# A fused Fourier mixing and SoLU block in fp32: a transform moved one step, the last units' sums and products moved to other engines

## The chip, the cores and the metric

The kernel runs on one core of one Trainium2 chip. The metric is device time in microseconds of one execution, the median over several runs. The five engines that appear are TensorE (PE, with its weight loads as PEld), VectorE (DVE), ScalarE (ACT), GpSimd (POOL) and SyncE (SP); SP only issues DMAs here.

## The reference

The reference mixes eight sequences of 3136 rows and 256 features with a two-dimensional Fourier transform, of which the real part is kept, and then applies an MLP with a SoLU activation and a layer norm. All is fp32.

```python
X = np.fft.fft(x, axis=1)             # x: (8, 3136, 256)
X = np.fft.fft(X, axis=2).real
h = X.reshape(25088, 256) @ w_in      # (256, 1024)
sm = softmax(h)                       # exp(h - max) / sum
solu = h * sm
ln = (solu - mean) / sqrt(var + 1e-6) * g_ln
out = ln @ w_out                      # (1024, 256)
```

## The kernel before

**Pairs and units.** Two sequences form a pair; there are four pairs. The row index of a sequence is split as 49 x 64. A first transform (`transform1`, L176) works over the 49, one piece of it for two of the 64 columns; its result z is written to a DRAM tile `zd` (`keep`, L215) and read back with other axes in the partitions as `g` (`turn`, L218: four DMAs for each group of five k1). A second transform (`transform2`, L226) makes for each of 25 values of k1 one unit; the k1 and 49 - k1 rows of the output come from the sum and the difference of two halves, called signs 1 and 0. A unit of k1 = 0 has one sign alone. So there are 100 units, numbered through: 25 to each pair.

**One unit.** `up` (L259) multiplies q (the second transform's result, copied by ACT at L242) with `Wi` on PE, in four matmuls of 512 columns, which are two records each in the profile (L264). DVE makes ev (`even`, L267) and then both signs' h with their maxima (`join`, L273); ACT takes the exponential (`expo`, L281), DVE the product h times exp (`product`, L289), ACT the squares for the variance (`square`, L296). DVE transposes in blocks of 32 (`turn_both`, L334, L336), and sixteen DMAs on SP carry the blocks to their places in `uT` (`move_blocks`, L358, L365), for two units at a time. The unit's small statistics follow on ACT (`stats`, L303) and as a power on POOL (`power`, L313, L316).

**Down projection.** The output of a unit with two signs is a product of a 2 x 2 block matrix with a 2 x 2 block matrix. Class `Down` (L403) computes it with seven block products of four 128-column matmuls each (`product7`, L398, L401) instead of eight. For this, four sums S of blocks of uT are formed on POOL (`sums`, L388, L394), about 1.3 us each, into one of two S tiles. The products lie in shared PSUM banks: C11 in bank 2, X in bank 3, the pair P4 and P5 in bank 1. `seed` (L426) copies C11 into X on ACT before p6 accumulates there; `keep_p`, `keep_x` and `keep_c` scale results out of the banks on ACT, and `finish` (L455) adds the rest on DVE. Units with one sign, the first units and the last unit use plain products with `Wo` instead (`down`, L462, L468) and a scale on ACT (L473). Results leave by one plain DMA on SP and, for sign 1, by one indirect DMA on POOL (`store`, L475).

**Order.** The program's order is written out by hand under a manual schedule; each engine runs its own instructions in that order. Units 0 to 4 (`whole = 4`) run in a first loop: the units before unit 4 are transposed by PE (`turn_whole`, L341), whose second half of PSUM copies is on DVE (L790). From unit 5 on, step i of the second loop holds `up` of unit i, the down projection of unit i - 5 (`lag = 5`), the sums of unit i - 4, and the elementwise work of unit i. After unit 99, steps 100 to 105 drain the pipeline. Bank 0 (L199, L233) serves the second transform and the first transform's pieces in turn, so a piece of `transform1` waits until ACT has copied q out.

**The next pair's work.** While pair p runs, `ahead` (L641) prepares pair p + 1. For each of eight chunks c it adds the mirrored rows on POOL in two halves (`add_mirror`, L128, L134), folds the features on DVE in two halves (`fold_part`, L156, L141, L142, L166) with a small copy on ACT (L167), and loads chunk c + 2 (`load`, L109: one DMA on SP at L117 and an indirect one on POOL at L119). `ahead_pe` puts two pieces of `transform1` per chunk on PE (L208). Chunk c's first mirrored half stands in step `SUMS[p][c]`, that is base + 2c with a base for each pair; the folds stand in that step + 1 and + 2, the load in + 2, and the pieces of the transform in + 3 and + 4. `turn_parts` (L664) reads the five groups of g at steps -4, -3, 2, 6 and 11 of the pair, on POOL's queue, into three buffers. The block moves of two units are issued in even steps, before that step's loads.

A mirrored sum and the first sum of S wait for the product of an earlier unit; `behind` adds that wait:

```python
def behind(i, t):
    tc.add_manual_dep(i.ins, t.last.ins.name, ...,
[...]
```

Of the kernel before, what the change touches and what calls it, by code (L numbers as in the profile page):

```python
# [26 lines left out]
NC = NH // CH  # L27
# [8 lines left out]
def kernel(  # L36
# [19 lines left out]
    nc = tc.nc  # L56
    B, S, D = x.shape
# [70 lines left out]
    def add_mirror(pr, c, engine, part=None):  # L128

        xa, xb, _ = pr.raw[c]  # L130
        rows = (0, CH) if part is None else (part * CH // 2, (part + 1) * CH // 2)
        r = slice(rows[0], min(rows[1], CH - 1 if c == NC - 1 else CH))
        a, rb = xa[:, r, :], xb[:, ::-1, :][:, r, :]
        i = engine.tensor_tensor(out=a[:, :, 1:D], in0=a[:, :, 1:D], in1=rb[:, :, D - 1 : 0 : -1], op=ALU.add)  # L134
        if part is None:
            engine.tensor_tensor(out=a[:, :, 0:1], in0=a[:, :, 0:1], in1=rb[:, :, 0:1], op=ALU.add)
        return i
# [143 lines left out]
    def expo(t, s):  # L281
        if s == 0:
            t.esum = small.tile([P, 2], FP32, tag="esum", name="esum")
            t.both = fpool.tile([P, 2, FF], FP32, tag="u", name="u", bufs=1)
        t.u[s] = t.both[:, s]
        nc.scalar.activation(out=t.u[s], in_=t.h[s], func=ACT.Exp, bias=t.nmax[:, s : s + 1], scale=-1.0,  # L286
                             accum_out=t.esum[:, s : s + 1])
# [8 lines left out]
    def square(t, s):  # L296

        if s == 0:
            t.ssq = small.tile([P, 2], FP32, tag="ssq", name="ssq")
        nc.scalar.activation(out=t.h[s], in_=t.u[s], func=ACT.Square, bias=t.usum[:, s : s + 1], scale=-float(FF),  # L300
                             accum_out=t.ssq[:, s : s + 1])
# [32 lines left out]
    def turn_both(t):  # L334
        if len(t.signs) == 2:
            nc.vector.transpose(out=t.batch.v[:, t.w].rearrange("p f o -> p o f"), in_=t.both)  # L336
        else:
            for s in range(2):
                turn_blocks(t, s)
# [45 lines left out]
    def blocks_of(t):  # L385
        return [S_tiles[t.w][:, j] for j in range(4)]

    def sums(t, prv):  # L388

        A11, A12, A21, A22 = blocks(t)  # L390
        S = blocks_of(t)
        for j, a, b, op in ((0, A21, A22, ALU.add), (1, S[0], A11, ALU.subtract), (3, A12, S[1], ALU.subtract),
                            (2, A11, A21, ALU.subtract)):
            i = nc.gpsimd.tensor_tensor(out=S[j], in0=a, in1=b, op=op)  # L394
            if j == 0 and prv:
                behind(i, prv)

# [238 lines left out]

    SUMS = [None] + [[f + 2 * c for c in range(NC)] for f in (3, 28, 53)]

    def ahead(pr, i, work):  # L641

        for c in range(NC):
            a = i - SUMS[pr.p][c]
            if work == "load" and (i == (pr.p - 1) * NK and c < 2 or a == 2 and c + 2 < NC):
                load(pr, c if a != 2 else c + 2)
            if work == "mirror" and a in (0, 1):
                behind(add_mirror(pr, c, nc.gpsimd, a), units[i - 1])
            if work == "fold" and a in (1, 2):
                fold_part(pr, c, a - 1)  # L650

    def behind(i, t):

        tc.add_manual_dep(i.ins, t.last.ins.name,
                          mybir.DependencyInfo(mybir.DependencyClass.Sync, mybir.DependencyReason.DATA),
                          reason="two operands at a time from SBUF")
# [7 lines left out]

    def turn_parts(pr, step):

        at = (-4, -3, 2, 6, 11)
        if step in at:
            turn(pr, at.index(step))

    with tc.manual_schedule():
# [71 lines left out]
        units = [Unit(p, k1) for p in range(NP) for k1 in range(NK)]  # L743
# [7 lines left out]
        lag = 5  # L751
        whole = 4
# [21 lines left out]
        def other_pairs(i, do, *a):  # L774
            cur = units[i]
            if cur.p + 1 < NP:
                do(pairs[cur.p + 1], i, *a)
# [3 lines left out]
        for i in range(whole + 1):  # L781
            cur = units[i]
            prv = units[i - 1] if i else None
            if prv:
                turn_whole(prv)
            for s in cur.signs:
                join(cur, s)
            if prv:
                for o, ps in prv.wait:
                    nc.vector.tensor_copy(out=o, in_=ps)  # L790
            for s in cur.signs:
                expo(cur, s)
            if i == 0:

                weights.narrow_out(3)
            for s in cur.signs:
                product(cur, s)
                if i < whole and s == 0:
                    square(cur, s)
            if i == 1:  # L800
                weights.centre()
                weight_sums()
            if i < whole:

                begin(i + 1)
                if 1 in cur.signs:
                    square(cur, 1)
                stats(cur)
                power(cur)
            else:  # L810
                for s in cur.signs:
                    square(cur, s)
                turn_both(cur)
                stats(cur)
                power(cur)
            if i == 0:
                turn(first, 1, nc.sync)
            for work in ("mirror", "fold", "load"):
                other_pairs(i, ahead, work)

        def by_seven(i):

            return 0 <= i < len(units) - 1 and len(units[i].signs) == 2

# [1 line left out]
        for i in range(whole + 1, len(units) + lag + 1):  # L828
            cur = units[i] if i < len(units) else None
            prv = units[i - 1] if whole < i - 1 < len(units) else None  # L830
            old = units[i - lag] if i < len(units) + lag else None
            seven = by_seven(i - lag)
            kept = units[i - lag - 1] if i >= lag + 1 else None

            if kept:
                store(kept, 0)
            if cur:
                enter(i)
                even(cur, up(cur, 0))
                cur.odd = up(cur, 1)  # L840
                second_transform(i + 2)
            if seven:
                new = Down(old, fresh)
                fresh = False
                new.p1()
                new.seed()
            if prv:
                stats(prv)
            if seven:
                new.p4()  # L850
                new.p5()
                new.keep_p()
            elif old:
                plain = [(s, down(old, s, result(s + 1)[:, 0:D])) for s in old.signs]
            if cur:
                other_pairs(i, ahead_pe)
            if seven:
                new.p6()
                new.keep_x()
                new.p2()  # L860
                new.keep_c()
            elif old:
                for s, ps in plain:
                    scale(old, s, ps)
            if cur:
                for s in cur.signs:
                    join(cur, s)
            if seven:
                new.p3()
                new.p7()  # L870
                new.finish()
            if cur:
                other_pairs(i, ahead, "mirror")
            if by_seven(i + 1 - lag):
                sums(units[i + 1 - lag], prv)
            if i % 2 == 0 and whole < i - 1 < len(units) - 2:
                batches[i // 2 - 1].place()
                move_blocks(batches[i // 2 - 1], slice(0, 2))
            if prv:
                power(prv)  # L880
            if kept and 1 in kept.signs:
                store(kept, 1)
            if cur:
                other_pairs(i, ahead, "fold")
                for s in cur.signs:
                    expo(cur, s)
                for s in cur.signs:
                    product(cur, s)
                for s in cur.signs:
                    square(cur, s)  # L890
                turn_both(cur)
                if cur.p == 0 and i in (5, 8, 11):
                    turn(first, (i + 1) // 3)
                for pr in pairs[1:]:
                    turn_parts(pr, i - pr.p * NK)
                other_pairs(i, ahead, "load")
            if i in (len(units), len(units) + 1):
                w = i - len(units)
                if w == 0:
                    batches[-1].place()  # L900
                move_blocks(batches[-1], slice(w, w + 1), (nc.sync, nc.gpsimd) if w else (nc.sync,))
# [76 lines left out]
```

## Time and profile before

| | us |
|---|---|
| median of 3 runs | 1172.91 |
| runs | 1169.1 to 1174.48 |
| the profiled execution | 1172.88 |
| its span | 1171.0 |
| PE busy | 1115.0 (95%) |
| DVE busy | 1022.6 (87%) |
| POOL busy | 868.2 (74%) |
| ACT busy | 757.5 (65%) |

The span begins with the first and ends with the last instruction of the profiled execution. Busy time counts an engine's instructions; in a line of the timeline stand the start, the duration, the engine, the line of the kernel, the operation, its tiles as out<-in, shapes and count, and in brackets the engine's idle time before it with what ended it. That last name is inferred, and of several causes the last one is named. In a line of windows stand the bounds, the length, each engine's busy time and count, the clock granted to TensorE as a share of full speed, the busy share of the DMA engines, and GB/s.

### The profile page before, as it was taken

Reading aid. Unit: us, or ns where it says so; the run is one execution under the profiler, and the core shown is the slowest. Engines: PE = TensorE matmul, PEld = TensorE weight load, DVE = VectorE, ACT = ScalarE, POOL = GpSimd, SP = SyncE. Lnnn points to the kernel's source line nnn. Section 1 sums busy time; section 2 is a strip of 40 time slices with the busy share of each in tenths; the row PEclk is TensorE's granted clock in tenths of the full one; section 3 lists DMA queues with packets and bytes.
Section 4 is the critical chain, followed back from the end, with each engine's and each line's share of the span. In section 5 each row is a group of like instructions: output and inputs, shape, how many; then the busy total and the mean of one; then the engine's idle time right before and its main releaser. Section 6 shows DMA issues by size and latency. Waiting matters only on the chain. (4 is left out here: it accounts for less than half of the span.)

```text
span 1171.0 us, 21594 instructions
## 1 busy us (share of the span) xinstructions
PE 1115.0 (95%) x7002; PEld 891.1 (76%) x7002; DVE 1022.6 (87%) x1428; ACT 757.5 (65%) x1721; POOL 868.2 (74%) x750
## 2 busy tenths in 40 slices
PE   2987999999999999999999999999999999999996
PEld 1555787787787777778878777878878788888886
DVE  7889989888999989999899999888898998998860
ACT  4566666667666666667666766676666666666651
POOL 3035888874998797887688889876598687777675
PEclk9999999999999989999999999999999999999998
DMA  9672798866897969886869797976596675956653
GB/s 240 197 190 45 168 186 186 196 144 145 157 182 155 186 149 174 170 174 143 161 133 202 156 190 164 205 174 144 134 168 154 130 161 113 165 120 134 137 120 93
DMA packets 458479, 185.75 MB, mean 159 GB/s; under 512 B 425750, under 2 KB 440350, under 8 KB 458368
## 3 DMA queue, kind: packets, MB, share of 16 engines
q1 hardware_dynamic: 444608, 146.22, 60.9%
q0 software_dynamic: 13760, 38.16, 12.5%
q8 instruction: 57, 0.93, 0.3%
q14 instruction: 54, 0.44, 0.1%
HBM read 44.78 MB, written 38.80 MB: 71 GB/s over the span
## 5 line engine op out<-in xcount | busy, mean ns | idle before, releaser
L264 PE MATMUL ps_h<-Wi,q 128*128 128x512 f32 x800 | 363.6, 596 | 11.4 <-DVE ev L270 5.9
L394 POOL TENSOR_TENSOR S<-uT 128x512 f32<-128x512 f32 x190 | 258.4, 1360 | 102.1 <-DMA r<-q 39.2
L300 ACT ACTIVATE h<-u,usum 128x1024 f32<-128x1024 f32 x196 | 225.2, 1149 | 155.8 <-DVE u L293 155.8
L401 PE MATMUL ps_m<-Ws,S 128*128 128x128 f32 x2280 | 297.3, 277 | 5.7 <-POOL S L394 3.3
L401 PEld LDWEIGHTS ps_m<-Ws,S 128*128 128x128 f32 x2280 | 280.0, 193 | 10.1 <-POOL S L394 3.7
L264 PEld LDWEIGHTS ps_h<-Wi,q 128*128 128x128 f32 x800 | 144.3, 191 | 160.0 <-issue 141.7
L293 DVE SCALAR_TENSOR_TENSOR u<-h,u 128x1024 f32<-128x1024 f32 x196 | 261.0, 1367 | 0.4 <-ACT u L286 0.3
L286 ACT ACTIVATE u<-h,nmax 128x1024 f32<-128x1024 f32 x196 | 223.7, 1143 | 19.3 <-DVE nmax L278 14.6
L336 DVE STREAM_TRANSPOSE v<-u 128x2048 f32<-128x2048 f32 x93 | 215.4, 2316 | 3.2
L401 PE MATMUL ps_m<-Wo,uT 128*128 128x128 f32 x1520 | 210.9, 282 | 0.0
L401 PEld LDWEIGHTS ps_m<-Wo,uT 128*128 128x128 f32 x1520 | 195.2, 197 | 0.9 <-issue 0.9
L394 POOL TENSOR_TENSOR S<-uT,S 128x512 f32<-128x512 f32 x95 | 134.9, 1420 | 7.4
L278 DVE CUSTOM_DVE_ANT_0 h<-ev,ps_h 128x1024 f32<-128x1024 f32 x100 | 122.1, 1221 | 18.1 <-DVE ev L270 7.4
L479 POOL DMA_INDIRECT out_dram<-ot,idx x96 | 115.6, 1204 | 29.4 <-issue 19.1
L394 POOL TENSOR_TENSOR S<-S,uT 128x512 f32<-128x512 f32 x95 | 129.1, 1359 | 7.5
L278 DVE CUSTOM_DVE_ANT_0 h<-h,ps_h 128x1024 f32<-128x1024 f32 x96 | 117.2, 1221 | 14.2 <-DVE nmax L278 0.5
L270 DVE SCALAR_TENSOR_TENSOR ev<-w_mid,r,ps_h 128x1024 f32<-128x1024 f32 x100 | 124.0, 1240 | 4.1 <-ACT S L530 2.6
L316 POOL TENSOR_TENSOR rs<-v,neg_half 128x2 f32<-128x2 f32 (+1 forms) x100 | 85.8, 858 | 32.3 <-ACT v L309 27.0
L401 PE MATMUL ps_m<-Ws,uT 128*128 128x128 f32 x760 | 105.0, 281 | 0.0
L208 PE MATMUL ps_m<-y,F 98*100 98x258 f32 (+3 forms) x288 | 73.8, 392 | 30.4 <-DVE y L154 23.1
L401 PE MATMUL ps_m<-Wo,S 128*128 128x128 f32 x760 | 100.9, 276 | 0.0
L236 PEld LDWEIGHTS ps_m<-T,g 128*128 128x128 f32 x400 | 60.2, 191 | 48.8 <-issue 46.0
(92 smaller groups left out, 1175.8 us busy)
## 6 DMA issues: line engine op xcount, KB each, us to landing
uT<-v SPq DMA_DIRECT2D x752, 128.0 KB
out_dram<-ot SPq DMA_DIRECT2D x100, 128.0 KB
g<-zd POOLq DMA_DIRECT2D x72, 160.0 KB, 5.2
xa<-in_x_dram SPq DMA_DIRECT2D x28, 392.0 KB
zd<-z SPq DMA_DIRECT2D x24, 400.0 KB
raw_in<-in_moe_w_in_dram SPq DMA_DIRECT2D x4, 512.0 KB
raw_out<-in_moe_w_out_dram SPq DMA_DIRECT2D x2, 1024.0 KB
r<-q SPq DMA_DIRECT2D x100, 0.5 KB
```

The costliest lines, as they stand in the source:

```text
L208: nc.tensor.matmul(o[..., cs], F[:, 2 * t + h, :], i[..., cs], start=first, stop=True, skip_group_check=True)
L264: nc.tensor.matmul(ps[:, fs], t.q[:, c * P : (c + 1) * P], Wi[:, c, fs], start=True, stop=True)
L270: nc.vector.scalar_tensor_tensor(out=t.ev, in0=w_mid, scalar=t.r, in1=ps, op0=ALU.mult, op1=ALU.add)
L278: nc.vector.tensor_tensor_reduce(out=t.h[s], in0=t.h[0] if s else t.ev, in1=t.odd, scale=1.0 if s else -0.5, scalar=3.0e38, op0=ALU.add, o ...
L286: nc.scalar.activation(out=t.u[s], in_=t.h[s], func=ACT.Exp, bias=t.nmax[:, s : s + 1], scale=-1.0, accum_out=t.esum[:, s : s + 1])
L293: t.last = nc.vector.scalar_tensor_tensor(out=t.u[s], in0=t.h[s], scalar=-1.0, in1=t.u[s], op0=ALU.mult, op1=ALU.mult, accum_out=t.usum[:, ...
L300: nc.scalar.activation(out=t.h[s], in_=t.u[s], func=ACT.Square, bias=t.usum[:, s : s + 1], scale=-float(FF), accum_out=t.ssq[:, s : s + 1])
L316: nc.gpsimd.tensor_tensor(out=t.rs[:, n], in0=t.v[:, n], in1=neg_half[:, n], op=ALU.pow)
L336: nc.vector.transpose(out=t.batch.v[:, t.w].rearrange("p f o -> p o f"), in_=t.both)
L394: i = nc.gpsimd.tensor_tensor(out=S[j], in0=a, in1=b, op=op)
L401: nc.tensor.matmul(o, a[:, c], b[:, c], start=start and c == 0, stop=c == n - 1, skip_group_check=True)
L479: dma = nc.gpsimd.indirect_dma_start(out=out, out_offset=bass.IndirectOffsetOnAxis(ap=idx[:, i : i + 1], axis=0), in_=t.ot[s], in_offset=None)
```

## The change

It has these parts.

- The base of the third pair in `SUMS` goes from 28 to 27, so that its mirrored sums, folds, transform pieces and loads (all but the first two) stand one step earlier.
- The third group of g is read at step 1 of each later pair instead of 2.
- In the first loop, at unit 4, the two PSUM copies of unit 3's sign 1 go from DVE to ACT, behind the exponentials, and the mirrored sum of that step goes ahead of the transpose and of `power`, and waits for unit 4's product instead of unit 3's.
- The squares of unit 99 go from step 99 into step 100, behind the seed of unit 95.
- The sums of units 97 and 98 go from POOL to DVE, and unit 99 is computed with the seven block products too, with its sums on DVE in step 103.

```diff
-    def sums(t, prv):
+    def sums(t, prv, engine=nc.gpsimd):
...
-            i = nc.gpsimd.tensor_tensor(out=S[j], in0=a, in1=b, op=op)
+            i = engine.tensor_tensor(out=S[j], in0=a, in1=b, op=op)
...
-    SUMS = [None] + [[f + 2 * c for c in range(NC)] for f in (3, 28, 53)]
-
-    def ahead(pr, i, work):
+    SUMS = [None] + [[f + 2 * c for c in range(NC)] for f in (3, 27, 53)]
+
+    def ahead(pr, i, work, after=None):
...
-                behind(add_mirror(pr, c, nc.gpsimd, a), units[i - 1])
+                behind(add_mirror(pr, c, nc.gpsimd, a), after or units[i - 1])
...
-        at = (-4, -3, 2, 6, 11)
+        at = (-4, -3, 1, 6, 11)
...
-            if prv:
+            if prv and i < whole:
                 for o, ps in prv.wait:
                     nc.vector.tensor_copy(out=o, in_=ps)
             for s in cur.signs:
                 expo(cur, s)
+            if prv and i == whole:
+                for o, ps in prv.wait:
+                    nc.scalar.copy(o, ps)
...
                 for s in cur.signs:
                     square(cur, s)
+                other_pairs(i, ahead, "mirror", cur)
                 turn_both(cur)
...
-            for work in ("mirror", "fold", "load"):
+            for work in ("mirror", "fold", "load") if i < whole else ("fold", "load"):
...
-            return 0 <= i < len(units) - 1 and len(units[i].signs) == 2
+            return 0 <= i < len(units) and len(units[i].signs) == 2
...
+            if i == len(units):
+                for s in prv.signs:
+                    square(prv, s)
             if prv:
                 stats(prv)
...
-                sums(units[i + 1 - lag], prv)
+                sums(units[i + 1 - lag], prv, nc.vector if i > len(units) else nc.gpsimd)
...
-                for s in cur.signs:
-                    square(cur, s)
+                if i < len(units) - 1:
+                    for s in cur.signs:
+                        square(cur, s)
                 turn_both(cur)
```

## The prediction

> **What bounds the kernel now.** I read the page first, then the starts of the matmuls of `up` (L264) in the timeline as a clock of the steps, then the waits, then single windows.
>
> ```profile
> PE 1115.0 (95%) x7002; PEld 891.1 (76%) x7002; DVE 1022.6 (87%) x1428; ACT 757.5 (65%) x1721; POOL 868.2 (74%) x750
> ```
>
> TensorE is the bound. By the starts of L264, a step takes 10.28 us, and 11.14 us where it also carries a piece of the next pair's first transform (11.60 with the last, three-part piece); a step that retires a single-sign unit takes 7.34 us. In such steps no PE wait stands in the timeline, so nothing that only relieves another engine pays there. What can pay are the steps that exceed these figures. They lie in three places: steps 5 and 6 (12.83 and 13.20 us), the transform of the third pair (step 33: 17.70, 38: 12.38, 39: 12.94, 40: 11.60, 43: 11.44), and the drain after unit 99.
>
> ```profile
> core 0: us, PE busy (x) PEld busy (x) DVE busy (x) ACT busy (x) POOL busy (x), PEclk, DMA share, GB/s
> ...
> 370.10:609.50 239.40, 232.06 (x1463) 186.97 (x1462) 218.64 (x301) 156.58 (x365) 187.22 (x158) 0.99 0.77 160
> 651.40:881.80 230.40, 228.27 (x1462) 184.06 (x1461) 208.25 (x301) 157.52 (x367) 183.71 (x159) 1.00 0.79 169
> ...
> 106.10:119.30 13.20, 13.20 (x75) 9.78 (x76) 12.62 (x18) 8.92 (x21) 12.56 (x13) 0.87 0.53 123
> ...
> 410.50:418.60 8.10, 7.55 (x37) 7.05 (x38) 5.29 (x7) 4.75 (x15) 7.61 (x7) 0.58 0.89 204
> ...
> 1146.90:1157.70 10.80, 8.08 (x58) 7.89 (x58) 0.83 (x2) 1.46 (x4) 9.39 (x11) 0.84 0.57 125
> ```
>
> The first two rows are the key: steps 30 to 50 and steps 55 to 75 do the same work for the third and the fourth pair (1463 and 1462 matmul records), yet the third pair needs 9.0 us more. The other rows show a granted clock (the number after POOL) far under 1.00: after a long PE wait the matmuls run slowly too. Step 33 in the timeline, SP, POOL, ACT and PE:
>
> ```profile
> 377.67 15.17 SPq L365 DMA_DIRECT2D uT<-v  x16
> 392.95 0.66 SPq L117 DMA_DIRECT2D xa<-in_x_dram  x1
> ...
> 400.74 1.26 POOL L134 TENSOR_TENSOR xa<-xa,xb 98x510 f32<-98x510 f32 x1 [6.43 <-DVE ot L457]
> ...
> 407.52 1.15 ACT L300 ACTIVATE h<-u,usum 128x1024 f32<-128x1024 f32 x1 [5.49 <-DVE u L293]
> ...
> 411.05 2.02 PE L208 MATMUL ps_m<-y,F 98*100 98x258 f32 x4 [3.33 <-ACT q L242]
> ```
>
> The load of x is queued on SP behind sixteen block moves of an even step, and is issued 15 us after them. POOL waits 6.43 us in front of the mirrored sum. I read this as a wait for that load: the engine named, DVE's L457, had ended 0.1 us before by chance, and at steps 36, 40 and 42 the same wait is put down to the load. Behind it in POOL's order stand the sums, so DVE's fold and product come late, then ACT's squares, then the copy of q that PE's L208 needs.
>
> [...] L166 takes 0.15 us alone (419.86) and 2.44 us against two mirrored sums (102.39). [...] the clock of 0.87 over 13.2 us is 3.4 us at half speed, 0.58 over 8.1 us is 6.8 us, 0.84 over 10.8 us is 3.5 us.
>
> **Third pair one step sooner (28 to 27).** Nothing is added or removed: 16 mirrored sums (1.28 us each on POOL), their folds, 16 pieces of transform, 6 later loads on SP and POOL and 8 writes of zd on SP move by one step; the first two loads stay in step 25. The loads of chunks 2 to 7 then fall in odd steps, where SP has no block moves, so they go out ahead of the next sixteen rather than behind them. That is how pairs two (base 3) and four (base 53) stand. Pair four's equal stretch is therefore my price: **239.4 - 230.4 = 9.0 us** less. The old excess by steps bounds it from above: 6.56 + 1.24 + 1.80 + 0.46 + 0.30 = 10.4. At the onset I charge 0.8 us: the g load and the first mirrored sum now stand ahead of step 27's sums, as they do at step 54 now (11.11 against 10.28). I give back 0.6: turn 0 of the next pair needs the last zd, which now lands a step earlier (steps 49 and 50 exceed 10.28 by 0.55 and 0.09). Sum 8.8, ends 4 and 11.
>
> **Load of g one step sooner.** Three times four DMAs, 2.4 us of POOL (637.43), go from steps 27, 52, 77 to 26, 51, 76. Their slot is free: the piece it held was last read at step 22 of the pair before. At step 51 they fill the 1.83 us that POOL waits for uT before 628.37, and the mirrored sum of step 53 starts about 2 us earlier, off DVE's products (2.23 and 2.31 us there, against 1.22 alone). Steps 54 and 55 exceed by 0.83 and 0.70. I take **0.6**, ends 0 and 1.5.
>
> **Unit 4.** Two PSUM copies (1.34 us together) leave DVE for ACT, where such a copy takes 0.61 us (L356), behind both exponentials; the mirrored sum goes behind unit 4's own product, so that it runs beside DVE's transpose, and ahead of power on POOL.
>
> ```profile
> 102.20 2.61 POOL L134 TENSOR_TENSOR xa<-xa,xb 98x510 f32<-98x510 f32 x2
> 102.39 2.44 DVE L166 TENSOR_TENSOR y<-xa,xb 98x2 f32<-98x2 f32 x1
> ...
> 106.07 5.43 PE L264 MATMUL ps_h<-Wi,q 128*128 128x512 f32 x8 [4.10 <-DVE ev L270]
> ```
>
> DVE gains 0.7 us at the product and 2.3 us at L166, so ev and PE's L264 come up to 2.9 us sooner and the half clock may go (1.7 us more). What is late next: unit 5's fold then meets POOL's four sums (about 104 to 109.5) from their first to their last, where now it meets only the end; in step 32 a fold amid sums took 4.9 us instead of 1.0. Product, squares, q copy and L208 of step 6 then come hardly sooner. ACT's copy of the bank that q needs delays PE's L236 by 0.8 us, hidden under the wait for ev. Ends -0.5 and 4; I take **0.8**.
>
> **The drain.** *Squares behind the seed:* p6 of unit 95 now waits 1.57 us, as the seed (L426) stands behind two squares on ACT. With the seed first, p6 and p2 follow p5 at once; p3 then waits for keep_p, still behind squares and stats (1131.3). So of 1.57 us I keep 0.85: unit 96 begins at 1133.3 instead of 1134.1.
>
> ```profile
> 1130.45 1.13 PE L401 MATMUL ps_m<-Ws,S 128*128 128x128 f32 x8 [1.57 <-issue]
> ...
> 1145.43 4.71 POOL L365 DMA_DIRECT2D uT<-v  x8
> ...
> 1151.71 3.44 PE L401 MATMUL ps_m<-Ws,S 128*128 128x128 f32 x16 [2.72 <-POOL S L394]
> ...
> 1157.72 7.08 PE L468 MATMUL ps_m<-Wo,uT 128*128 128x256 f32 x32
> ...
> 1167.12 0.96 POOL L479 DMA_INDIRECT out_dram<-ot,idx  x1 [2.18 <-issue]
> ```
>
> *Sums on VectorE:* twelve sums come to DVE, which is idle here. [...] L141's 688 ns at 508 elements agrees. Four cost about 2.8 us, against 5.1 on POOL. They stand behind the unit before's finish, so the first is ready some 0.3 us before the next p5 asks. The wait of 2.72 us for unit 98, caused by eight DMAs on POOL ahead of its sums, goes, and with it 1.5 us of half clock. Units 96, 97 and 98 take 6.4 us each (1134.14 to 1140.54): 1133.3 + 19.2 = 1152.5.
>
> *Unit 99 in block products:* 28 products of 128 columns in 6.4 us replace 7.08 us of plain ones, and the two scales behind them. Its block moves on SP (0.9 us each, from about 1142.7) end near 1150.2 and land in 3 us, so p1 may wait some 0.5. p7 ends at 1159.3, the finish (0.48) at 1159.8, the last indirect store starts at 1160.0. From the start of that store to the end the profile now has 1171.0 - 1167.12 = 3.9 us, which gives 1163.9: **7.1 us** less. Ends 4 (late block moves, a store held by the one before: these start 3.1 to 5.1 us apart) and 8.5.
>
> **Sum.** 8.8 + 0.6 + 0.8 + 7.1 = 17.3 us. The profiled execution took 1172.88 us (span 1171.0), the median is 1172.91, so no correction: **1155.6 us**. A measurement can tell about 0.5%, 5.9 us, from no change.
>
> **Rivals.** *More:* the third pair loses all 10.4, unit 4's half clock goes (4), the drain gives 8: 1150. [...] Chance 0.15. *A new wait in the third pair:* odd steps put the g load and an x load both into step 31, 3.4 us of POOL, and POOL's mirror, sums, power and store already fill 8.8 to 10 of 11.14; [...]: 1161. For: step 59 exceeds by 0.80, three steps after such a load. Against: step 61 has both and exceeds by nothing. Chance 0.17. *The third pair's load is hidden as badly as before,* and only the drain pays: 1166, a fifth of it within 0.5%. Chance 0.05. *Slower:* in the third pair L208 waits over 3.3 us and the clock halves, in several places; one such event cost 6.56 us (step 33). With 10.4 of old excess removed and 8.5 from the rest, 18.9/6.56 = 2.9: from three events on the change doesn't pay, and four give 1180. For: DVE and POOL are at 87% and 74%. Against: in steps 57 to 71, with the same parity, L208's longest wait is 0.56 us. Chance 0.04. The likeliest case has 0.57; the last 0.02 ends within 0.5%.
>
> **Range.** 1149 to 1163.5 takes in the likeliest, *more* and most of the *new wait*.
>
> **What would show it.** Step 33 at 11.14 and no POOL wait for xa in steps 31 to 42; steps 30 to 50 near 230 us; L394 on DVE twelve times near 0.69 us; no half clock between 1130 us and the last product; the last store some 3.9 us before the end. It is wrong if L208 waits over 1 us in the third pair, or if DVE's sums of unit 97 hold up p5.

## The result, and the profile after

The changed kernel takes 1158.4 us (median of 4 runs, 1157.45 to 1159.71) against 1171.01 for the kernel before beside it (4 runs, 1167.31 to 1174.48): a ratio of 0.9894 with a 95% interval of 0.9857 to 0.993, so 12.6 us faster. A second set of runs gave 1158.95 against 1171.92, ratio 0.989 (0.9871 to 0.9909). The forecast was 1155.6. The profiled execution took 1157.6 us, its span is 1155.8: 15.2 us less than the profiled execution of before.

The busy times, first section of the page after:

```profile
PE 1109.1 (96%) x7026; PEld 888.2 (77%) x7026; DVE 1013.8 (88%) x1440; ACT 758.3 (66%) x1725; POOL 848.0 (73%) x742
```

TensorE is still the bound. DVE has twelve instructions more on balance (twelve sums and two for unit 99's finish came, two PSUM copies went) and is still 8.8 us less busy: its folds are shorter (L141 and L142 together fall from 70.4 to 58.2 us), which I put down to fewer of them running beside POOL's instructions. Windows of the kernel after, with the columns as before: step 6; steps 28 and 29; steps 30 to 50; and from the start of step 99 to the end.

```profile
104.03:118.41 14.38, 11.95 (x75) 9.35 (x76) 13.77 (x16) 9.11 (x22) 13.74 (x14) 1.00 0.48 112
348.56:373.69 25.13, 22.61 (x138) 18.46 (x137) 23.99 (x30) 14.83 (x36) 22.12 (x17) 0.93 0.85 165
373.69:601.20 227.51, 227.46 (x1462) 183.93 (x1461) 202.07 (x295) 156.45 (x364) 177.59 (x156) 1.00 0.76 164
1107.21:1155.80 48.59, 42.49 (x346) 40.04 (x344) 26.18 (x40) 17.62 (x44) 26.25 (x28) 0.98 0.55 127
```

In the third row PE is busy for all but 0.05 us of 227.5. The second row is where the loss sits: two steps that took 20.56 us before take 25.13, at a clock of 0.93. Cut at the starts of L264, the two kernels, each profiled twice, compare so (us; "again" is the same kernel in a later set of runs):

| steps | before | before again | after | after again |
|---|---|---|---|---|
| start and 0 to 4 | 93.25 | 93.35 | 94.19 | 94.02 |
| 5, 6 | 26.02 | 25.70 | 24.22 | 24.23 |
| 7 to 26 | 219.98 | 219.69 | 219.87 | 221.55 |
| 27 to 29 | 30.84 | 30.84 | 35.41 | 35.40 |
| 30 to 50 | 239.37 | 238.99 | 227.51 | 227.52 |
| 51 to 56 | 62.36 | 63.54 | 62.79 | 62.46 |
| 57 to 98 | 444.28 | 444.62 | 443.22 | 444.14 |
| 99 to the end | 54.91 | 53.59 | 48.62 | 48.31 |

*Third pair.* The chain that ended in step 33 before ends in step 32 now (timeline of after, SP, POOL and PE: the load of x, the block moves, the mirrored sum that needs this load, and L208 of step 32):

```profile
375.18 0.36 SPq L117 DMA_DIRECT2D xa<-in_x_dram  x1
...
381.27 13.51 SPq L365 DMA_DIRECT2D uT<-v  x16
...
387.05 1.27 POOL L134 TENSOR_TENSOR xa<-xa,xb 98x510 f32<-98x510 f32 x1 [0.31 <-DVE u L293]
...
399.99 1.03 PE L208 MATMUL ps_m<-y,F 98*100 98x258 f32 x4
```

The load is issued 6.1 us ahead of the sixteen block moves instead of after them, the mirrored sum waits 0.31 us instead of 6.43, and L208 does not wait. Every step from 32 to 44 takes 11.14 or 11.15 us. Steps 28 and 29 show the price of it (timeline of after, POOL, DVE, ACT and PE):

```profile
345.10 2.41 POOL L224 DMA_DIRECT2D g<-zd  x4
...
347.52 1.30 POOL L134 TENSOR_TENSOR xa<-xa,xb 98x510 f32<-98x510 f32 x1
...
358.99 1.52 POOL L394 TENSOR_TENSOR S<-uT 128x512 f32<-128x512 f32 x1
...
360.81 1.51 DVE L142 TENSOR_TENSOR y<-xa 98x254 f32<-98x254 f32 x1
...
362.24 1.26 DVE L166 TENSOR_TENSOR y<-xa,xb 98x2 f32<-98x2 f32 x1
...
364.56 2.05 DVE L293 SCALAR_TENSOR_TENSOR u<-h,u 128x1024 f32<-128x1024 f32 x1
364.67 1.15 ACT L300 ACTIVATE h<-u,usum 128x1024 f32<-128x1024 f32 x1 [3.49 <-DVE u L293]
...
368.05 0.27 ACT L426 COPY ps_m<-ps_m 128x128 f32<-128x128 f32 x1
...
368.42 1.54 PE L401 MATMUL ps_m<-Ws,S 128*128 128x128 f32 x8 [2.49 <-issue]
...
369.75 1.92 PE L401 MATMUL ps_m<-Wo,uT 128*128 128x128 f32 x8
```

From the g load at 345.10 POOL has hardly a gap until 366. Its four sums of step 28 (358.99 to 365.5) therefore fall on DVE's fold (L142 1.51 us instead of 0.41, L166 1.26 instead of 0.15) and on the second product (2.05 instead of 1.22). ACT's squares wait 3.49 us for that product, the seed behind them comes at 368.05, and p6 on PE, put down to "issue", waits 2.49 us for the seed. Then eight products take 1.92 us instead of 1.10: the granted clock is 0.50 for 3.4 us, from 368.97 on.

*Unit 4* (timeline of after, POOL, DVE and PE):

```profile
99.81 1.27 POOL L134 TENSOR_TENSOR xa<-xa,xb 98x510 f32<-98x510 f32 x1 [2.64 <-DVE u L293]
...
102.63 0.16 DVE L166 TENSOR_TENSOR y<-xa,xb 98x2 f32<-98x2 f32 x1
...
104.03 1.98 PE L264 MATMUL ps_h<-Wi,q 128*128 128x512 f32 x4 [0.32 <-DVE ev L270]
...
107.54 1.51 DVE L142 TENSOR_TENSOR y<-xa 98x254 f32<-98x254 f32 x1
...
113.84 1.11 PE L208 MATMUL ps_m<-y,F 98*100 98x258 f32 x4 [1.55 <-ACT q L242]
```

L166 takes 0.16 us where it took 2.44, and L264 waits 0.32 us where it waited 4.10, at a granted clock of 1.00: step 5 falls from 12.83 to 9.84 us. The next fold then meets POOL's sums, and L208 waits 1.55 us: step 6 rises from 13.20 to 14.38.

*Drain* (timeline of after, PE, DVE, ACT and POOL):

```profile
1122.48 1.13 PE L401 MATMUL ps_m<-Wo,S 128*128 128x128 f32 x8 [0.67 <-ACT ot L435]
...
1138.54 0.69 DVE L394 TENSOR_TENSOR S<-S,uT 128x512 f32<-128x512 f32 x1
...
1142.67 0.37 ACT L444 ACTIVATE ot<-ps_m,rs 128x128 f32<-128x128 f32 x1 [1.94 <-DMA out_dram<-ot,idx]
...
1143.09 1.16 PE L401 MATMUL ps_m<-Ws,S 128*128 128x128 f32 x8 [0.28 <-ACT ot L444]
...
1151.93 0.95 POOL L479 DMA_INDIRECT out_dram<-ot,idx  x1 [2.63 <-DVE ot L459]
```

No product waits for a sum any more. A new wait stands at L444 in unit 98: ACT waits 1.94 us for an earlier indirect store to free the output tile. Here PE notices 0.28 us of it.

### The profile page after: what moved, and what is told of

It reads as the page before. It is cut to its first block, busy times and chain, and to the rows that moved or that the text cites. A ratio compares the mean times of both kernels' runs of the same rounds, so it can differ in the third digit from the quotient of the medians.

```text
span 1155.8 us, 21664 instructions
## 1 busy us (share of the span) xinstructions
PE 1109.1 (96%) x7026; PEld 888.2 (77%) x7026; DVE 1013.8 (88%) x1440; ACT 758.3 (66%) x1725; POOL 848.0 (73%) x742
## 4 chain that ended last, share of the span: by engine, by line
PE 81%; DMA 5%; SPq 4%; DVE 4%; issue 2%; POOL 2%; ACT 1%; POOLq 0%; DVEq 0%; ACTq 0%
PE ps_m L401 48%; PE ps_h L264 25%; PE ps_m L208 4%; PE ps_m L236 3%; SPq L365 3%; DMA room<-in_x_dram 2%; DMA uT<-v 1%; DVE h L278 1%; POOL S L394 1%; DMA r<-q 1%; DVE u L293 1%; DMA F<-in_f_tab_dram 1%; SPq L216 1%; PE ps_m L468 1%; PE wps L601 1%
## 5 line engine op out<-in xcount | busy, mean ns | idle before, releaser
L264 PE MATMUL ps_h<-Wi,q 128*128 128x512 f32 x800 | 362.0, 594 | 7.9 <-DVE nmax L278 4.8
L394 POOL TENSOR_TENSOR S<-uT 128x512 f32<-128x512 f32 x186 | 251.1, 1350 | 104.6 <-DMA out_dram<-ot 40.9
L264 PEld LDWEIGHTS ps_h<-Wi,q 128*128 128x128 f32 x800 | 144.0, 190 | 155.3 <-issue 139.9
L278 DVE CUSTOM_DVE_ANT_0 h<-ev,ps_h 128x1024 f32<-128x1024 f32 x100 | 122.1, 1221 | 17.3 <-DVE ev L270 7.9
L479 POOL DMA_INDIRECT out_dram<-ot,idx x96 | 111.2, 1158 | 33.5 <-issue 16.6
L394 POOL TENSOR_TENSOR S<-S,uT 128x512 f32<-128x512 f32 x93 | 126.6, 1362 | 7.3
L316 POOL TENSOR_TENSOR rs<-v,neg_half 128x2 f32<-128x2 f32 (+1 forms) x100 | 78.2, 782 | 28.4 <-ACT v L309 27.0
L236 PEld LDWEIGHTS ps_m<-T,g 128*128 128x128 f32 x400 | 60.1, 191 | 49.4 <-issue 45.8
L401 PEld LDWEIGHTS ps_m<-Ws,uT 128*128 128x128 f32 x768 | 98.0, 196 | 0.0
```

The lines of the kernel that those rows point to most:

```text
L236: nc.tensor.matmul(o, g[:, k, h * P : (h + 1) * P], table, start=(h == 0), stop=True, skip_group_check=True)
L264: nc.tensor.matmul(ps[:, fs], t.q[:, c * P : (c + 1) * P], Wi[:, c, fs], start=True, stop=True)
L278: nc.vector.tensor_tensor_reduce(out=t.h[s], in0=t.h[0] if s else t.ev, in1=t.odd, scale=1.0 if s else -0.5, scalar=3.0e38, op0=ALU.add, o ...
L316: nc.gpsimd.tensor_tensor(out=t.rs[:, n], in0=t.v[:, n], in1=neg_half[:, n], op=ALU.pow)
L394: i = engine.tensor_tensor(out=S[j], in0=a, in1=b, op=op)
L401: nc.tensor.matmul(o, a[:, c], b[:, c], start=start and c == 0, stop=c == n - 1, skip_group_check=True)
```

## The experiments

Each kernel is the changed kernel with the edit shown, apart from the two repeats. In all the expectations, O is the theory that at the onset of the third pair POOL is late because the load of g stands right ahead of the first mirrored sum; F is its rival, that the fold meets POOL's sums there whatever the load of g does; Q is the theory that the old waits of the third pair come from SP's queue, since the load of x stands behind the block moves; S is its rival, that what helps is the step of slack itself, wherever the loads stand. One-execution figures are segments of the profiled execution, cut as in the table above; where a median is given, several runs stand behind it.

### What the moved base is worth: base 28 again

```diff
-    SUMS = ... for f in (3, 27, 53)]
+    SUMS = ... for f in (3, 28, 53)]
```

> The changed kernel with the third pair's base back at 28; all else stays changed. In the profile of the changed kernel the third pair lost 4.6 us at its onset (steps 28 and 29) and won 11.9 us in steps 31 to 50. Theory Q (the loads of x stand in SP's queue behind sixteen block moves when they fall in even steps) and rival S (what helps is the step of slack itself, wherever the loads stand) both expect the third pair's stalls back: step 33 near 17.7 us, 38 and 39 over 12, steps 28 and 29 at 10.28, and 1157.6 + 7.3 = 1165 us in all. If it stays at 1158, the base had no part in the gain. It is the control for the run with loads on POOL's queue.

Measured: median 1162.98, ratio 0.9926 (0.9903 to 0.9948), against 0.9894 of the changed kernel; the difference is 0.0032, or 3.7 us, but the two intervals overlap, so the segments have to carry the reading. By segments, 31.45 + 237.26 for steps 27 to 50 against 35.41 + 227.51: the earlier base wins 9.75 and loses 3.96 at the onset, 5.8 net. SP and POOL of this kernel:

```profile
375.79 14.00 SPq L365 DMA_DIRECT2D uT<-v  x16
389.90 0.83 SPq L117 DMA_DIRECT2D xa<-in_x_dram  x1
...
397.78 1.26 POOL L134 TENSOR_TENSOR xa<-xa,xb 98x510 f32<-98x510 f32 x1 [4.69 <-DVE nmax L278]
```

The wait of 4.69 us is back, and with it the excess of steps 33, 34, 37 to 40 and 43. But step 33 takes 12.92 us, not the 17.70 of before (17.77 in the repeat): relative to the start of step 33 the load is issued 1.9 us earlier than in the kernel before (9.85 against 7.96 us ahead of it), L208 waits 1.5 instead of 3.33 us, and the half clock does not come. Of the 4.8 us by which step 33 is shorter, 1.8 are the shorter wait, and the other 3.0 I put down to the clock, which in the kernel before is 0.50 for 6.8 us from 410.55 on. Why the load goes out sooner here was not tested.

### Is it SP's queue? Base 28 with the loads of x on POOL

```diff
-        nc.sync.dma_start(out=xa, in_=x_pn[r, ...])
+        (nc.gpsimd if pr.p == 2 and c > 1 else nc.sync).dma_start(out=xa, in_=x_pn[r, ...])
```

(the base is 28 as in the last one)

> As the control (base 28, all else changed), but the third pair's loads of xa for chunks 2 to 7 are issued from POOL's queue beside their indirect twin, not from SP's. They stay in even steps. Theory Q: past the block moves, the loads land before the mirrored sums ask, POOL's wait in front of the mirrored sum at step 32 (6.4 us) goes, step 33 comes to 11.14 and steps 38 to 40 to 11.14; six DMA issues of 0.6 us on POOL cost up to 2 us; 1165 - 10 + 1 = 1156 us, range 1153 to 1158. Rival S: the slack is missing still, so 1164 to 1166.

Measured: median 1162.52, ratio 0.992 (0.9893 to 0.9946). This is a miss: Q expected 1153 to 1158 us, S 1164 to 1166, and neither came. The waits for xa in steps 32 and 36 to 42 are gone, as Q says, but steps 30 to 50 come down only from 237.26 to 234.83. POOL, DVE and PE in steps 37 and 38 of this kernel:

```profile
451.20 2.43 POOL L224 DMA_DIRECT2D g<-zd  x4
453.62 0.59 POOL L117 DMA_DIRECT2D xa<-in_x_dram  x1
454.51 1.06 POOL L119 DMA_INDIRECT xb<-in_x_dram,idx  x1 [0.30 <-issue]
455.60 1.27 POOL L134 TENSOR_TENSOR xa<-xa,xb 98x510 f32<-98x510 f32 x1
...
457.14 1.49 DVE L141 TENSOR_TENSOR y<-xa 98x254 f32<-98x254 f32 x1
...
465.93 1.11 PE L208 MATMUL ps_m<-y,F 98*100 98x258 f32 x4 [2.68 <-ACT q L242]
```

Now the issues themselves, 4.1 us of them in a row, put POOL's sums under DVE's fold (L141 1.49 us instead of 0.41), and step 38 takes 14.07 us. What stalls PE is that POOL comes late. The queue was one cause of that, and issues on POOL are another. This run alone does not rule out S. The kernel before speaks against it: the fourth pair's base stands as far behind its pair's start (53 - 50) as the third's (28 - 25), so it has no more slack, and yet its stretch, with the loads in odd steps, is 9.0 us shorter.

### The load of g at step 4, at step 3, and on SP's queue

```diff
-        at = (-4, -3, 1, 6, 11)
+        at = (-4, -3, 4, 6, 11)
```

> The changed kernel with the third group of g read at step 4 of each later pair (29, 54, 79) instead of 1; step 4 is where no sums are formed, as unit 25 (50, 75) has one sign. Theory O for the loss at the onset of the third pair (the g load and the first mirrored sum together make POOL late, so that the sums of step 28 meet DVE's fold and product, and the squares, seed and p6 wait): POOL is 2.4 us earlier in steps 26 to 28, step 29 falls from 14.59 to 10.3 to 11.5 and step 53 from 11.39 to 10.3; 1157.6 - 4.5 = 1153 us, range 1152 to 1155. Rival F (the fold of step 28 is one more instruction set than DVE has room for in a 10.28 us step, whatever POOL does): step 29 stays above 13, 1157 to 1159.

Measured: median 1156.2, ratio 0.9877 (0.9842 to 0.9912). Step 29 falls from 14.59 to 11.23 us without a half clock: O holds for most of the loss there. But step 31 rises from 11.43 to 13.67. POOL, DVE and PE in step 31:

```profile
377.15 1.50 POOL L394 TENSOR_TENSOR S<-uT 128x512 f32<-128x512 f32 x1 [2.09 <-DMA r<-q]
...
380.23 1.52 DVE L142 TENSOR_TENSOR y<-xa 98x254 f32<-98x254 f32 x1
...
386.54 1.11 PE L208 MATMUL ps_m<-y,F 98*100 98x258 f32 x4 [1.24 <-ACT q L242]
```

The sums of the step wait for a transfer and then meet the fold. The view names r, which the sums do not read; by the trace's semaphores the last of the sixteen block moves, issued at 369.43, landed at 376.99, just ahead of the sum. Of the 4.6 us lost in steps 28 and 29, 3.6 come back, and 2.2 are lost again in step 31.

```diff
+        at = (-4, -3, 3, 6, 11)
```

> The changed kernel with the third group of g read at step 3 of each later pair (28, 53, 78): behind the sums of that step in POOL's order and ahead of step 4, which forms no sums. With the load at step 4 the wait of step 29 went (14.59 to 11.23), but the load then stood ahead of step 30's mirrored sum and sums, and step 31 rose from 11.43 to 13.67. Theory O (any POOL work right ahead of a step's sums makes them meet DVE's fold and product): at step 3 the empty place in step 4 takes it up, step 29 near 11.2 and step 31 near 12.2, steps 27 to 31 together near 52.2 us against 55.0; 1155 to 1157 us, the best yet. Rival: the x loads of step 25 and the two mirrored sums alone cost what is left, and the place of the g load no longer matters: step 29 at 14 or more, or step 31 at 13.5.

Measured: median 1157.27, ratio 0.9859 (0.9835 to 0.9882); steps 29 and 31 take 11.25 and 13.67 us, the same as with step 4. The expectation that step 3 spares step 31 failed: whether the load stands in step 28 or in step 29 of the program makes no difference to step 31.

```diff
-        at = (-4, -3, 1, 6, 11)
+        at = (-4, -3, 2, 6, 10) if pr.p % 2 else (-4, -3, 1, 5, 11)
...
-            turn(pr, at.index(step))
+            turn(pr, at.index(step), nc.gpsimd if step < 0 else nc.sync)
```

> The changed kernel with the third, fourth and fifth group of g read from SP's queue, in odd steps (27, 31, 35; 51, 55, 61; 77, 81, 85), not from POOL's; the first two groups, which wait for the last writes of zd, stay on POOL. Theory O (what is left of the third pair's loss is POOL made late by its own DMA issues, so that the sums meet DVE's fold and product): POOL loses 2.4 us in each of nine steps, the third pair's steps 27 to 31 come from 55.0 us to 51 to 52, step 53 from 11.39 to 10.3, step 57 stays 11.14; some 5 us less than the changed kernel on the same chip, 1151 to 1154 us. Rival F (the fold does not fit into steps of 10.28 us): steps 28 and 29 still exceed 24.5 us together and the time is within 1.5 us of the changed kernel. Rival B: SP's queue holds the g load behind sixteen moves and PE waits for g, at transform2 ten or more steps on: slower.

Measured: median 1159.77, ratio 0.9889 (0.9872 to 0.9906), beside 1158.95 of the changed kernel on the same chip. Steps 29 and 31 take 11.26 and 12.20, so steps 27 to 31 are 2.8 us shorter than in the changed kernel. The medians show no gain. In the profiled execution the start up to step 5 was 2.0 us longer, and the finish was long: the last store started at 1151.86, as early as in the changed kernel, and the span ended 7.7 us later instead of 3.9.

Rival B did not happen: L236, which reads g, has no wait put down to it.

In all three, step 29 still has about 1 us over 10.28. F is right for that rest. With base 27 the first fold stands in step 28, amid the sums of unit 24; with base 28 it stands in step 29, which forms no sums, as unit 25 has one sign. DVE in the run with g at step 4, and in that with base 28:

```profile
359.01 1.52 DVE L142 TENSOR_TENSOR y<-xa 98x254 f32<-98x254 f32 x1
360.45 0.99 DVE L166 TENSOR_TENSOR y<-xa,xb 98x2 f32<-98x2 f32 x1
```

```profile
369.90 0.41 DVE L142 TENSOR_TENSOR y<-xa 98x254 f32<-98x254 f32 x1
370.23 0.15 DVE L166 TENSOR_TENSOR y<-xa,xb 98x2 f32<-98x2 f32 x1
```

### Unit 4 as before

```diff
-            if prv and i < whole:
+            if prv:
...
-            if prv and i == whole:
-                for o, ps in prv.wait:
-                    nc.scalar.copy(o, ps)
...
-                other_pairs(i, ahead, "mirror", cur)
...
-            for work in ("mirror", "fold", "load") if i < whole else ("fold", "load"):
+            for work in ("mirror", "fold", "load"):
```

> The changed kernel with unit 4 as before: the two PSUM copies on DVE, the mirrored sum behind the transpose and power. Steps 5 and 6 take 24.22 us together in the changed kernel and 26.02 in the one before. My account: L166 waits for the mirrored sums on POOL, ev of unit 5 is late, PE waits 4 us and runs at half clock: step 5 at 12.8, step 6 at 13.2. Rival: the half clock falls by chance; then step 5 is 12.8 and step 6 is 11.5, and the edit gains nothing.

Measured in one execution: steps 5 and 6 take 26.72 us against 24.22, with a wait of 4.1 us at L264 and a half clock of 6.8 us. In the kernel before it was 26.02 and 25.70, with 3.4 us. So the part is worth 1.5 to 2.5 us, depending on how long the half clock lasts.

### The drain as before

```diff
-            return 0 <= i < len(units) and len(units[i].signs) == 2
+            return 0 <= i < len(units) - 1 and len(units[i].signs) == 2
...
-            if i == len(units):
-                for s in prv.signs:
-                    square(prv, s)
...
-                sums(units[i + 1 - lag], prv, nc.vector if i > len(units) else nc.gpsimd)
+                sums(units[i + 1 - lag], prv)
...
-                if i < len(units) - 1:
-                    for s in cur.signs:
-                        square(cur, s)
+                for s in cur.signs:
+                    square(cur, s)
```

> The changed kernel with the drain as before: unit 99's squares ahead of the seed, the sums of units 97 and 98 on POOL, unit 99 by plain products. From the start of up of unit 99 to the end the changed kernel takes 48.6 us, the one before 54.9. My account expects 54.9 here, so 1157.6 + 6.3 = 1164 us, with unit 98's wait of 2.7 us for the sums and a half clock back. Rival: part of the 6.3 us is only the stretch before, which came earlier and changed the DMA traffic; then less than 5 us.

Measured: median 1161.3, ratio 0.9905 (0.9877 to 0.9934). The drain takes 54.02 us against 48.62. The old wait returns, with a half clock: sixteen products take 3.64 us instead of 1.95 (PE of this kernel):

```profile
1142.15 3.64 PE L401 MATMUL ps_m<-Ws,S 128*128 128x128 f32 x16 [2.22 <-POOL S L394]
```

The medians differ by 2.9 us and the ratios by 0.0011, less than the 5.4 of the segments; the repeats below come back to this.

### The three parts of the drain, each undone alone

Sums on POOL again (unit 99's too):

```diff
-                sums(units[i + 1 - lag], prv, nc.vector if i > len(units) else nc.gpsimd)
+                sums(units[i + 1 - lag], prv)
```

> The changed kernel with the sums of units 97, 98 and 99 on POOL again; unit 99 still by block products, squares still behind the seed. Measured from the start of up of unit 99 to the end (48.6 us in the changed kernel, 54.9 before). My account: the eight block moves on POOL stand ahead of the sums of unit 98 again, p5 of unit 98 waits 2 to 3 us and a half clock follows, and unit 99's sums come 5 us after those; 53 to 55 us. Rival: POOL is early enough now, since the rest moved 0.9 us ahead; under 51 us.

Measured in one execution: the drain takes 55.68 us, more than before the change; a product of S waits 3.03 us for its sum and the clock halves: sixteen products take 3.43 us instead of 1.95.

Unit 99 with plain products:

```diff
-            return 0 <= i < len(units) and len(units[i].signs) == 2
+            return 0 <= i < len(units) - 1 and len(units[i].signs) == 2
```

> The changed kernel with unit 99 by plain products again (so no sums for it), the sums of units 97 and 98 on DVE, squares behind the seed. From the start of up of unit 99 to the end: plain products of unit 99 start at the same place as its block products did, and took 13.3 us from there to the end before, against 11.75 in the changed kernel: 50.1 us. Rival: nothing is gained by block products at the end, as its finish on DVE and the store come last in either case; 48.6 us or less.

Measured in one execution: 48.72 us against 48.62 and 48.31, where I expected a loss. PE, ACT and POOL of this kernel:

```profile
1142.27 7.08 PE L468 MATMUL ps_m<-Wo,uT 128*128 128x256 f32 x32
...
1149.39 0.47 ACT L473 ACTIVATE ot<-ps_m,rs 128x256 f32<-128x256 f32 x1 [2.93 <-PE ps_m L468]
...
1150.14 0.96 POOL L479 DMA_INDIRECT out_dram<-ot,idx  x1 [2.81 <-ACT ot L473]
```

From unit 99's first product to its last store it is 7.87 us here, and 1151.93 - 1144.08 = 7.85 us in the changed kernel. The plain products take longer on PE, but one scale on ACT follows them; after the block products a finish on DVE does, and the store starts 0.8 us after that ends.

Squares ahead of the seed again:

```diff
-            if i == len(units):
-                for s in prv.signs:
-                    square(prv, s)
...
-                if i < len(units) - 1:
-                    for s in cur.signs:
-                        square(cur, s)
+                for s in cur.signs:
+                    square(cur, s)
```

> The changed kernel with unit 99's squares ahead of the seed of unit 95 again. My account: p6 of unit 95 waits 1.57 us instead of p3 waiting 0.67, and all behind it ends 0.9 us later: 49.5 us from the start of up of unit 99 to the end. Rival: p3 is held by keep_p in any order, so nothing changes, 48.6 us.

Measured in one execution: 49.80 us; p6 waits 1.57 us again. Against 48.62 that is 1.2 us more. As executions of one drain differ (see below), the fairer partner is one with as long a wait at L444 (2.0 us, 48.69 in all), and gives 1.1.

### Both kernels again

> The changed kernel again, as the partner of the run with g on SP: 1158 us within 1 us, steps 28 and 29 together 24 to 25.2 us in the profile, if the loss at the onset is no accident of one execution.

> The kernel before, profiled a second time, to see how much of my 9.0 us for the third pair was one execution's. With base 28 and everything else changed, step 33 took 12.92 us without a half clock, where the first profile of the kernel before had 17.70 with one. If the half clock of step 33 is an accident, steps 30 to 50 take 232 to 237 us here, not 239.4, and step 33 under 14.5. If it belongs to the kernel before, 238 to 240 us again and step 33 over 16.

The changed kernel: 1158.95, as at first; the onset repeats to 0.02 us (14.57 in step 29). The kernel before, one run: 1172.09, with 17.77 us in step 33 and 238.99 in steps 30 to 50. Both stalls belong to the programs. The half clock at the onset does not always: the runs with the old drain and with the sums on POOL have the same code for the third pair, step 29 takes 12.99 and 13.02 us there at the full clock, and step 31 12.19 instead of 11.43.

The same drain code stands in eight of the profiled executions, and it took 48.62, 48.31, 48.99, 52.26, 48.69, 53.27, 52.01 and 50.10 us, 50.3 in the mean; the old drain took 54.91, 53.59 and 54.02, 54.2 in the mean. Its mean worth is thus 3.9 us, and the profiled execution of the changed kernel lay at the good end. Most of the spread goes with one wait, that of ACT for the output tile at L444 in unit 98: 1.62 us in the execution of 48.31, 1.94 in that of 48.62, then 2.01, 2.30 and 3.40, in the order of their drains. In the one of 53.27 the end after the last store was long. With the load of g at step 3 the drain took 52.01, and the view of ACT and PE there shows why:

```profile
1142.02 0.37 ACT L444 ACTIVATE ot<-ps_m,rs 128x128 f32<-128x128 f32 x1 [3.77 <-DMA out_dram<-ot,idx]
...
1142.44 1.16 PE L401 MATMUL ps_m<-Ws,S 128*128 128x128 f32 x8 [2.11 <-ACT ot L444]
1143.44 1.77 PE L401 MATMUL ps_m<-Wo,uT 128*128 128x128 f32 x8
```

The wait for the output tile at L444 is 3.77 us instead of 1.94, PE waits 2.11 and the clock halves: eight products take 1.77 us instead of 1.11. The execution with the loads of x on POOL shows the same, 3.79 and 2.13 us.

## Why the prediction was right or wrong

The direction and the bottleneck were right, and the time lies in the range, 2.8 us above the forecast. That it lies so close is in part luck, as the sum below shows: three of the four terms were too high, one too low.

- **Third pair, 8.8 forecast, 7.3 in the profiles (270.21 to 262.92).** The mechanism went as written: step 33 at 11.14, no POOL wait for xa in steps 31 to 42. In the kernel before, the trace has the load of 392.95 landing at 400.57, just ahead of the mirrored sum at 400.74, so the wait was read rightly. The price by the fourth pair's stretch was too small: with the 0.6 of steps 49 and 50, which both take 10.28 now (and took it in the repeat of the kernel before, so this excess was one execution's), it gave 9.6, and steps 30 to 50 fell by 11.9. That is more than the excess of the five steps, 10.4, and the 0.6 together: step 31 lost another 0.90 (12.33 to 11.43), which I hadn't counted. A twin with stalls of its own is a poor price: the third pair's stretch is now 2.9 us shorter than the fourth's of before.
- **The onset, 0.8 forecast, 4.6 measured.** This is the step that failed. It was priced by step 54, where the g load and the first mirrored sum stood ahead of one step's sums. That twin lacked what costs here. The fourth pair's first fold meets no sums, as step 54 of the program forms none (unit 50 has one sign): in the kernel before, L142 takes 0.41 us there (653.10) and L166 0.15. Base 27 moves the third pair's first fold into step 28, amid four sums. That leaves about 1 us even with the g load out of the way (11.2 in step 29, with the load at step 3, at step 4 or on SP). The g load at step 1 makes POOL later still, the second product meets the last sum too, PE waits 2.5 us, and step 29 comes to 13.0, or to 14.6 when the clock halves. With base 28 the same g load costs next to nothing (10.48). Each part was costed alone, and the rival "a new wait in the third pair" looked for the meeting in step 31, where g load and x load do meet without harm (11.43). Base 27 with the g load at its old place, step 2, was not run, so how much the base would cost by itself is not shown.
- **Load of g, 0.6 forecast, nothing found.** Steps 51 to 56 took 62.36 and 63.54 before, 62.79 and 62.46 after. Step 54 did fall from 11.11 to 10.35 (11.33 to 10.33 in the repeats), but step 53 rose from 10.28 to 11.39 (10.92 to 11.06). And it brings most of the onset: away from there, 3.6 of the 4.6 us in steps 28 and 29 are gone.
- **Unit 4, 0.8 forecast, 1.8 measured (26.02 to 24.22).** The mechanism went as written, the early L264 and the next fold amid POOL's sums. I had counted on little of the half clock's share, and all of it went (step 6 now runs at 1.00).
- **Drain, 7.1 forecast, 6.3 in the profiles and 3.9 in the mean of executions.** The sums on DVE take 0.68 to 0.71 us, in line with the 688 ns of L141 for 508 elements. The squares are worth 1.1 to 1.2 (0.85 forecast), p3 then waits 0.67 for keep_p as said, and from last store to end it is 3.9 us as said. Not seen was the output tile: L444 in unit 98 waits for an earlier store, between 1.6 and 3.8 us; what sets the length of that wait stays open. The block products of unit 99 give nothing: what they save on PE, the finish and the start of the store take back.

In the profiles, -7.3 + 0.4 - 1.8 - 6.3 is 15.0 of the 15.2. With the drain's mean in place of 6.3 it is 12.6, and the medians say 12.6 and 13.0. Against the 17.3 of the sum 4.7 us are missing: 3.8 at the onset, 3.2 in the drain and 1.0 of the g load, less 2.3 more in the third pair and 1.0 more at unit 4. The median is nevertheless only 2.8 us off, as the kernel before ran at 1171.01 here and not at the 1172.91 that I subtracted from. That the drain's spread also explains the small difference of the medians with the old drain is argued from the segments, not shown.

Open stays why step 31 slows down when step 29 is quick. With base 27 the two went against each other: 14.6 us in step 29 with 11.43 in step 31, 13.0 with 12.19, and 11.25 with 13.67 (12.20 with g on SP). A quick step 29 leaves the sixteen block moves less time before the sums of step 30 ask for them, which would fit the wait seen with g at step 4 (with g on SP there is none), but this was not tested, and neither was a version that frees both steps. The best version seen puts the load of g at step 3 (0.9859, or 0.9877 with step 4); its interval overlaps that of the changed kernel.

## What to carry to other kernels

A twin gives a price only if its step has the same neighbours: the onset of the fourth pair looked like that of the third, but had no sums beside its first fold. When two moved steps land on the same queue within one step of each other, cost them together: the g load cost next to nothing with base 28, and with base 27 it brought 3.6 us. An engine that is only 73% busy on average, as POOL is here, can have no slack for 20 us, and where an engine that takes longer beside it (DVE's L142 1.51 us instead of 0.41) leads to the bottleneck, that stretch decides. At the end of a kernel, look for the output tiles and the stores behind the products before making the products shorter.

## What the hardware showed beyond this

In the trace of the kernel before, the granted clock is 0.50 for 3.4 us from 106.76 on, for 6.8 us from 410.55 on and for 3.4 us from 1151.24 on; in that of the changed kernel it is 0.50 for 3.4 us from 368.97 on. The same wait did not always bring a half clock. Seven profiled executions have the code of the changed kernel in the third pair, and in step 29 of each p6 waits 2.48 to 2.50 us. In five of them the clock halved (step 29 takes 14.59 us in the changed kernel), in two it did not (12.99 and 13.02 us). PE in one of these two, the run with the old drain:

```profile
368.62 1.13 PE L401 MATMUL ps_m<-Ws,S 128*128 128x128 f32 x8 [2.48 <-issue]
```

In the profiles of the two kernels, past the first 60 us, a half clock came with the PE waits of 4.10, 3.33, 2.72 and 2.49 us, and none with that of 2.06 (at 79.28 in the changed kernel) or with those of 1.57 and less. In the other executions shown here it came with waits of 3.03, 2.22, 2.13 and 2.11 us, and not with those of 2.48 (above) and of 2.68 (at 465.93 with the loads of x on POOL). So a wait of 2 to 3 us costs its own length, or by my estimate 1.7 us more (half of 3.4 us), and one execution doesn't tell which.

DVE's fold took longer amid POOL's sums, and each of its instructions did so anew: a fold of three takes 1.0 us alone (0.41, 0.41 and 0.15) and 4.2 us amid four sums of POOL (1.49, 1.50 and 1.25, with the loads of x on POOL). The small one suffers most for its size, from 0.15 to 1.25 us. What holds them up is not shown by the traces.
